# The MLP's first layer as Strassen's block product on one Trainium2 core

## Chip, cores and metric

The kernel runs on one core of a Trainium2 chip. Times are microseconds (us) of the device, from one launch of the whole program. Lower is better.

## What is computed

Three layers run one after the other. Attention of 8 batches, 8 heads and 576 rows against pooled keys and values gives x of 4608 tokens by 512. A mixture of 8 experts (each token goes to one) maps x to y of the same shape. The last layer is the MLP, which is what the change is about:

```python
def _moe2_ref(x, w_in, w_out):          # x 4608 x 512, w_in 512 x 2048, w_out 2048 x 512
    h = x @ w_in
    g = h * (1.0 / (1.0 + np.exp(-h)))
    return (g @ w_out).astype(np.float32)
```

The weights of the MLP come as 64-bit floats; everything else is 32-bit.

## The kernel before, in words

Every product of two numbers in these matmuls is taken in three: an operand is split into a high part (`fp32r`, a copy by ScalarE) and a low part (the difference, by VectorE), and hi x hi, lo x hi and hi x lo are added up in PSUM.

**Mixture stage** (`run_items`, line 990): 16 items of one, two or three blocks of 128 tokens (`ORDER`), 120 units in all. Its program order is written out by hand. SP loads the experts' weights; between the units, `decode_ops` (line 200) is drained step by step from a list: 32 chunks of the MLP's 64-bit weights are loaded, put together as 32-bit numbers on VectorE, ScalarE and GpSimd, and split. The 16 chunks of `w_in` come first and go to SBUF tiles `wi` (high and low, line 818). The 16 chunks of `w_out` go through two stores each (lines 277, 278) to the DRAM tensors `wod`. At unit `PREP` = 112 `prepare_y` (line 1280) frees the decoder's memory, loads the first block's input (`load_y(0)`), and `trans_y` (line 947) transposes it on VectorE and splits it.

**MLP stage** (from line 1299): 12 blocks of 384 tokens (`TB`), each with 16 units (one per 128 columns of `w_in`). `c1` (line 1326) computes 128 columns of h for the block with 12 matmuls of 384 columns into one of three PSUM banks, then sigmoid (ScalarE), product (VectorE), high part (ScalarE), low part (VectorE). `c2` (line 1348) multiplies them by the unit's rows of `w_out`: 9 matmuls of 512 columns into three PSUM banks that collect a block's 16 units. `c_out` (line 1360) copies the rows out of PSUM and scatters them to `out`. The `w_out` parts are loaded from `wod` when the stage starts (line 1381), with the second block's input between them (`YF`). `load_y` (line 937) brings a block's 384 rows by four transfers of short runs; it is called one block ahead at the least, and `trans_y` runs in units 8 to 11 of the block before. SP and GpSimd follow the program's order (line 1300); the order on the other engines is a planner's.

Of the kernel before, what the change touches and what calls it, by code (L numbers as in the profile page):

```python
# [8 lines left out]
F32 = mybir.dt.float32  # L9
F32R = mybir.dt.float32r  # L10
# [33 lines left out]
YF = 5  # L44
# [4 lines left out]
HOLD = 2  # L49
# [68 lines left out]
def kernel(  # L118
# [76 lines left out]
    wod = [tc.dram_tile([DFF, DM], F32, name=f"wod{i}") for i in range(2)]  # L195
# [4 lines left out]
    def decode_ops(pctx, wi):  # L200
# [3 lines left out]
        def chunk(src, hi, lo, nm, after):  # L204
# [30 lines left out]

            def out_hi():
                if hi is None:
                    st["hi"] = dp.tile([P, 512], F32R, tag="hi", name=f"hi_{nm}", bufs=2)
                    st["lo"] = st["A"].bitcast(F32R)
                else:  # L240
                    st["hi"], st["lo"] = hi, lo
                nc.scalar.copy(out=st["hi"], in_=st["A"])

            def rest():
                nc.gpsimd.tensor_tensor(
                    out=st["A"] if wide else st["lo"], in0=st["A"], in1=st["hi"].bitcast(F32), op=ALU.subtract
                )
# [15 lines left out]
            if wide:  # L263
                ops.append(
                    lambda: nc.gpsimd.tensor_tensor(out=st["lo"], in0=st["A"], in1=st["B"], op=ALU.add)
                )
# [3 lines left out]
        for c in range(DM // P):  # L270
            for f in range(DFF // 512):
                fs = slice(f * 512, f * 512 + 512)
                chunk(w_in[c * P : (c + 1) * P, fs], wi[0][c][:, fs], wi[1][c][:, fs], f"i{c}_{f}", None)
        for f in range(DFF // P):

            def after(hi, lo, f=f):
                nc.sync.dma_start(out=wod[0][f * P : (f + 1) * P, :], in_=hi.bitcast(F32))
                nc.sync.dma_start(out=wod[1][f * P : (f + 1) * P, :], in_=lo.bitcast(F32))

            chunk(w_out[f * P : (f + 1) * P, :], None, None, f"o{f}", after)  # L280
# [537 lines left out]
    wi = [[wip.tile([P, DFF], F32R, tag=f"wi{i}_{c}", name=f"wi{i}_{c}") for c in range(DM // P)] for i in range(2)]  # L818
# [115 lines left out]
    yin, yT, g_t, o_t, ypool = {}, {}, {}, {}, []  # L934
    NB = N // TB

    def load_y(b):
        if b >= NB:
            return
        yin[b] = ypool[b % 2].tile([P, 4, TB], F32, tag="yin", name=f"yin{b}", bufs=1)  # L940
# [6 lines left out]
    def trans_y(b, c, pool, tag):  # L947
        if b >= NB:
            return
        if c == 0:  # L950
            yT[b] = [ypool[b % 2].tile([P, 4, TB], F32R, tag=t, name=f"{t}{b}", bufs=1) for t in ("yh", "yl")]
        yf = pool.tile([P, TB], F32, tag=tag, name=f"yf{b}", bufs=3)
        nc.vector.transpose(out=yf, in_=yin[b][:, c, :])
        yh, yl = yT[b]
        nc.scalar.copy(out=yh[:, c, :], in_=yf)
        nc.vector.tensor_tensor(out=yl[:, c, :], in0=yf, in1=yh[:, c, :].bitcast(F32), op=ALU.subtract)

    bctx = ExitStack()
    with bctx:
# [296 lines left out]
        dq = decode_ops(dctx, wi)  # L1256
# [23 lines left out]
        def prepare_y():  # L1280
            assert not dq, len(dq)
            dctx.close()
            ypool.append(ctx.enter_context(tc.tile_pool(name="y0", bufs=1, side="right")))
            load_y(0)
            nc.scalar.activation(out=spacer, in_=spacer, func=AF.Sigmoid)

        pre[PREP] = [prepare_y]
        for c in range(4):
            pre[PREP + 3 + c] = [lambda c=c: trans_y(0, c, bp, "ys")]
# [8 lines left out]

    mctx.close()
    mctx.enter_context(tc.manual_schedule(engines={mybir.EngineType.SP, mybir.EngineType.Pool}))  # L1300
    ctx.enter_context(mctx)
    with ExitStack() as cctx:
        wop = cctx.enter_context(tc.tile_pool(name="wop", bufs=1, reuse_waits=RW))
        cp = cctx.enter_context(tc.tile_pool(name="cp", bufs=2, reuse_waits=RW))
        pch = cctx.enter_context(tc.tile_pool(name="pch", bufs=3, space=PSUM, reuse_waits=RW))
        pco = cctx.enter_context(tc.tile_pool(name="pco", bufs=5, space=PSUM, reuse_waits=RW))
        ypool.append(cp)
        NS = TB // P
        NF = DFF // P
# [16 lines left out]
        def c1(u):  # L1326
            b, f = divmod(u, NF)
            if b >= NB:
                return
            yh, yl = yT[b]  # L1330
            ps = pch.tile([P, TB], F32, tag="h", name=f"ch{u}")
            k = 0
            sl = slice(f * P, (f + 1) * P)
            for c in range(4):
                for w, x in ((wi[0], yh), (wi[0], yl), (wi[1], yh)):
                    nc.tensor.matmul(ps, w[c][:, sl], x[:, c, :], start=(k == 0), stop=(k == 11))  # L1336
                    k += 1
            sg = cp.tile([P, TB], F32, tag="sg", name=f"sg{u}")
            nc.scalar.activation(out=sg, in_=ps, func=AF.Sigmoid)  # L1339
            g = cp.tile([P, TB], F32, tag="g", name=f"g{u}")  # L1340
            nc.vector.tensor_tensor(out=g, in0=ps, in1=sg, op=ALU.mult)  # L1341
            gh = cp.tile([P, TB], F32R, tag="gh", name=f"gh{u}", bufs=3)
            gl = cp.tile([P, TB], F32R, tag="gl", name=f"gl{u}", bufs=3)
            nc.scalar.copy(out=gh, in_=g)  # L1344
            nc.vector.tensor_tensor(out=gl, in0=g, in1=gh.bitcast(F32), op=ALU.subtract)  # L1345
            g_t[u] = (gh, gl)

        def c2(u, cols=range(NS)):
            b, f = divmod(u, NF)
            gh, gl = g_t[u]  # L1350
            if f == 0:
                o_t[b] = [pco.tile([P, DM], F32, tag="o", name=f"o{s}_{b}") for s in range(NS)]
            for s in cols:
                sl_ = slice(s * P, (s + 1) * P)
                for k, (h, w) in enumerate(((gh, wo[0][f]), (gh, wo[1][f]), (gl, wo[0][f]))):
                    nc.tensor.matmul(  # L1356
                        o_t[b][s], h[:, sl_], w, start=(f == 0 and k == 0), stop=(f == NF - 1 and k == 2)
                    )

        def c_out(b, cols=range(NS)):  # L1360
            for s in cols:
# [69 lines left out]
```

## Time and profile before

| what | us |
|---|---|
| runs of the kernel | 1554.3, 1549.18, 1558.97 (median 1554.3) |
| the profiled execution | 1554.01 |
| its span, first to last instruction | 1552.1 |
| its mean granted TensorE clock | 0.966 |

The profile is of one execution. Its page sums up each engine's busy time, shows the span in 40 slices, and follows back the chain of work that ended last. The trace behind it can be asked for groups of instructions, for single instructions in order of time, and for the engines' busy time in a stretch. TensorE appears twice: PE are the matmuls, PEld the loads of their stationary operands, which overlap them. DVE is VectorE, ACT ScalarE, POOL GpSimd, SPq the queue of SyncE. A matmul's row lasts longer than its share of the engine, because matmuls are pipelined.

### The profile page before, as it was taken

How to read it: one execution, taken by the hardware profiler on the slowest of the kernel's cores; microseconds unless marked ns; L12 is line 12 of the kernel's file. 1: busy time of each engine (PE TensorE's matmuls, PEld its weight loads, DVE VectorE, ACT ScalarE, POOL GpSimd, SP SyncE). 2: the span in 40 equal slices, each digit the busy share in tenths (PEclk: the TensorE clock that was granted, in tenths of full speed). 3: DMA queues.
4: the chain of work that ended last, by engine and by line, in shares of the span. 5: the costliest groups of instructions: out<-in, count | busy, mean ns of one | idle time of the engine just before them, and what ended most of it. 6: DMA issues, size and time to landing. Idle time of an engine off the chain costs nothing.

```text
span 1552.1 us, 21780 instructions
## 1 busy us (share of the span) xinstructions
PE 1482.7 (96%) x8163; PEld 1328.5 (86%) x8164; DVE 784.2 (51%) x1454; ACT 603.6 (39%) x1250; POOL 375.9 (24%) x445
## 2 busy tenths in 40 slices
PE   8898876899999999999999999999999999999996
PEld 6788865788889899898889989998999999999996
DVE  6466456497888887884332323323232332323232
ACT  4555442355656555653222322322232232322221
POOL 1773034254345553531110101011010100100000
PEclk9989587999999999999999999999999999999998
DMA  9996014677658887883920102102020220000000
GB/s 256 271 250 119 28 68 132 206 241 226 233 188 276 280 295 253 296 252 91 234 41 1 41 1 41 20 22 42 1 41 1 41 32 10 21 1 21 0 21 21
DMA packets 231206, 179.12 MB, mean 115 GB/s; under 512 B 155032, under 2 KB 187803, under 8 KB 230450
## 3 DMA queue, kind: packets, MB, share of 16 engines
q1 hardware_dynamic: 218626, 147.31, 35.8%
q0 software_dynamic: 11456, 28.48, 5.2%
q8 instruction: 66, 1.08, 0.3%
q10 hardware_dynamic: 1008, 1.84, 0.3%
q14 instruction: 50, 0.41, 0.1%
HBM read 140.55 MB, written 37.83 MB: 115 GB/s over the span
## 4 chain that ended last, share of the span: by engine, by line
PE 76%; issue 7%; DMA 7%; DVE 5%; ACT 1%; another core or an unknown queue 1%; SPq 1%; POOL 1%; DVEq 0%; POOLq 0%; ACTq 0%
PE o L1356 23%; PE ch L1336 23%; PE pv L483 4%; DMA yd<-ys_-1_14_8004,rk 2%; PE sc L446 2%; PE psp L468 2%; DMA r_-1_2_2964<-in_moe_w_dram 1%; PE vw L409 1%; DMA xd<-xg 1%; DMA qz<-in_q_dram 1%; DMA gid<-idd,rowi 1%; PE warm L665 0%; DVE sg_i L226 0%; DMA yin<-yd 0%
## 5 line engine op out<-in xcount | busy, mean ns | idle before, releaser
L1336 PE MATMUL ch<-yh,wi 128*128 128x384 f32 x1536 | 398.0, 338 | 2.5 <-DVEq L1291 2.5
L1356 PE MATMUL o<-wo,gh 128*128 128x512 f32 x1152 | 357.6, 395 | 2.1 <-ACT gh L1344 2.1
L1341 DVE TENSOR_TENSOR g<-ch,sg 128x384 f32<-128x384 f32 x192 | 106.8, 556 | 419.7 <-ACT sg L1339 419.4
L1336 PEld LDWEIGHTS ch<-yh,wi 128*128 128x128 f32 x1536 | 282.5, 189 | 19.4 <-POOL spacer L1163 2.9
L1339 ACT ACTIVATE sg<-ch 128x384 f32<-128x384 f32 x192 | 94.5, 492 | 459.6 <-PE ch L1336 447.9
L1336 PE MATMUL ch<-yl,wi 128*128 128x384 f32 x768 | 259.8, 338 | 0.0
L1356 PEld LDWEIGHTS o<-wo,gh 128*128 128x128 f32 x1152 | 214.0, 188 | 37.0 <-ACT gh L1344 2.4
L1356 PE MATMUL o<-wo,gl 128*128 128x512 f32 x576 | 223.5, 396 | 0.0
L1366 POOL DMA_INDIRECT out_dram<-os,ids x33 | 32.5, 985 | 643.6 <-DVE os L1364 638.9
L1345 DVE TENSOR_TENSOR gl<-g,gh 128x384 fp32r<-128x384 f32 x192 | 106.8, 556 | 95.4 <-ACT gh L1344 92.2
L1336 PEld LDWEIGHTS ch<-yl,wi 128*128 128x128 f32 x768 | 145.0, 189 | 1.9
L1344 ACT CAST gh<-g 128x384 fp32r<-128x384 f32 x192 | 98.5, 513 | 112.9 <-DVE g L1341 107.9
L1356 PEld LDWEIGHTS o<-wo,gl 128*128 128x128 f32 x576 | 108.3, 188 | 25.3
L483 PE MATMUL pv<-vb,pT 72*128 72x128 f32 (+1 forms) x640 | 89.7, 295 | 2.8 <-DVE gh L517 1.9
L483 PEld LDWEIGHTS pv<-vb,pT 72*128 72x128 f32 (+1 forms) x640 | 82.0, 200 | 5.6 <-issue 2.7
L462 ACT ACTIVATE pe<-sc,nm 128x72 f32<-128x72 f32 x288 | 67.9, 320 | 8.8 <-DVE nm L456 8.5
L472 ACT COPY pT<-psp 72x512 f32<-72x512 f32 x72 | 42.0, 583 | 69.0 <-PE psp L468 54.7
L456 DVE TENSOR_REDUCE nm<-sc 128x4 f32<-128x288 f32 x72 | 32.4, 451 | 53.6 <-PE sc L446 30.4
L468 PE MATMUL psp<-ident,pe 128*72 128x128 f32 x288 | 49.4, 300 | 10.6 <-ACT pT L472 7.1
L446 PE MATMUL sc<-kbd,qT 128*128 128x144 f32 (+1 forms) x320 | 54.8, 316 | 1.5 <-issue 1.4
L564 POOL DMA_INDIRECT idd<-idw,sli x36 | 36.9, 1024 | 73.9 <-DVE idw L601 66.7
L446 PEld LDWEIGHTS sc<-kbd,qT 128*128 128x128 f32 (+1 forms) x320 | 43.9, 199 | 5.6 <-issue 3.6
(3518 smaller groups left out, 2688.2 us busy)
## 6 DMA issues: line engine op xcount, KB each, us to landing
yin<-yd SPq DMA_DIRECT2D x44, 192.0 KB
xd<-xg SPq DMA_DIRECT2D x32, 256.0 KB
raw_i<-in_moe_w_in_dram SPq DMA_DIRECT2D x16, 512.0 KB
raw_o<-in_moe_w_out_dram SPq DMA_DIRECT2D x16, 512.0 KB
wo<-wod SPq DMA_DIRECT2D x32, 256.0 KB
qz<-in_q_dram SPq DMA_DIRECT2D x28, 288.0 KB
kv<-in_k_dram SPq DMA_DIRECT2D x9, 768.0 KB
kv<-in_v_dram SPq DMA_DIRECT2D x6, 768.0 KB
```

The lines of the kernel that those rows point to most:

```text
L446: nc.tensor.matmul(ps[o : o + n, 2 * c : 2 * c + 2, :], qT_t[t][:, 2 * hf + c, o : o + n], kbds[b // 2 % 2][:, h0 : h0 + 5 : 4, :], start= ...
L462: nc.scalar.activation(out=pe[:, h * NK : h * NK + NK], in_=ps[:, h, :], func=AF.Exp, bias=nm[:, h, :])
L468: nc.tensor.transpose(ps[:, j, :], pe[:, NK * j : NK * j + NK], ident)
L472: nc.scalar.copy(out=pT_t[u], in_=ps_t.pop(u))
L483: nc.tensor.matmul(pv_t[t][o : o + n, j % 2, VW * c : VW * c + VW], pT[:, j, o : o + n], vw[b][:, HG * h : HG * h + VW], start=True, stop= ...
L564: ins = nc.gpsimd.indirect_dma_start(out=idd, out_offset=bass.IndirectOffsetOnAxis(ap=sli[:, i, :], axis=0), in_=idw[:, t, :], in_offset=None,
L1336: nc.tensor.matmul(ps, w[c][:, sl], x[:, c, :], start=(k == 0), stop=(k == 11))
L1339: nc.scalar.activation(out=sg, in_=ps, func=AF.Sigmoid)
L1341: nc.vector.tensor_tensor(out=g, in0=ps, in1=sg, op=ALU.mult)
L1344: nc.scalar.copy(out=gh, in_=g)
L1345: nc.vector.tensor_tensor(out=gl, in0=g, in1=gh.bitcast(F32), op=ALU.subtract)
L1356: nc.tensor.matmul(o_t[b][s], h[:, sl_], w, start=(f == 0 and k == 0), stop=(f == NF - 1 and k == 2))
```

## The change

Two blocks of 384 tokens form a superblock. In its product with `w_in` both are cut in two along the 512 inputs (b11, b21 of the first block, b12, b22 of the second), and `w_in` into four quarters of inputs by hidden columns (a step n takes the 128 columns n and the 128 columns n + 8). Eight quarter products of 6 matmuls give the four parts of h of a step; Strassen's product in Winograd's form gives them with seven, from sums of the quarters of `w_in` and of the transposed tokens (t1 to t4), and five additions per step on VectorE.

- Decoding: the parts of `w_in` go to SBUF tiles `em` and by 8 stores of 1.05 MB to DRAM (`wid`). Of `w_out` the high part stays in SBUF (`woh`), the low part is stored (`wold`).
- `prepare_y` also loads the first two steps' parts of `w_in` and of `w_out`'s low part. The first block is transposed there and split (b11, b21).
- First superblock: 16 steps j, block by block, two hidden columns each, with the eight products ("Q"). In the first eight, VectorE forms the sums s1 to s4 of the step's quarters, which are split and stored to DRAM (`wis`).
- Later superblocks: 8 steps n of seven products. Loads: "A" three quarters of `w_in` and "S" four sums, 786 KB and 1.05 MB a step, and two low parts of `w_out`, each in two buffers.
- The second layer's turn of a hidden part (`second`, the 9 matmuls) is taken from a list `pend`, a few products after the part's own.
- PSUM: banks a and b for the products (one buffer each) and six for the rows of out.
- The order is the program's on every engine.

The core of the diff:

```diff
-YF = 5
-HOLD = 2
+        def quarters(n):
+            w = wt["Q", n].bitcast(F32)
...
+            nc.vector.tensor_tensor(out=W4, in0=parts[0], in1=parts[1], op=ALU.add)
...
+            nc.vector.tensor_tensor(out=s1, in0=a21, in1=a22, op=ALU.add)
+            nc.vector.tensor_tensor(out=s3, in0=a11, in1=a21, op=ALU.subtract)
+        def sums(n):
...
+            nc.vector.tensor_tensor(out=s2, in0=s1, in1=a11, op=ALU.subtract)
+            nc.vector.tensor_tensor(out=s4_, in0=a12, in1=s2, op=ALU.subtract)
...
+            nc.scalar.copy(out=em[:, :, 0, :], in_=s4)
+            nc.vector.tensor_tensor(out=em[:, :, 1, :], in0=s4, in1=em[:, :, 0, :].bitcast(F32), op=ALU.subtract)
+            nc.sync.dma_start(
+                out=wis[n * P : (n + 1) * P, :], in_=em.rearrange("p o i x -> p (o i x)").bitcast(F32)
+            )
+        def product(ps, kind, o, n, nm, first):
+            w, (xh, xl) = wt[kind, n], X[nm, 0 if kind == "Q" else n // NFP]
             k = 0
+            for c in range(2):
+                for i, x in ((0, xh), (0, xl), (1, xh)):
+                    nc.tensor.matmul(
+                        ps, w[:, o, i, c, :], x[:, c, :], start=(first and k == 0), stop=(k == 5), skip_group_check=True
+                    )
+                    k += 1
...
+                (1, 2, load_y, b0), (2, 1, load_ids, b0), (2, 1, load_ids, b1), (2, 2, turn_y, b0, 0), (2, 2, turn_y, b0, 1),
+                (3, 1, turn_y, b0, 2), (3, 1, turn_y, b0, 3), (3, 2, load_y, b1), (4, 2, turn_y, b1, 0),
+                (4, 2, turn_y, b1, 1), (5, 1, turn_y, b1, 2), (5, 1, turn_y, b1, 3), (5, 2, sum_y, "t1", sb),
+                (6, 1, sum_y, "t2", sb), (6, 1, sum_y, "t3", sb), (6, 2, split_y, "b11", sb), (7, 1, sum_y, "t4", sb),
+                (7, 2, split_y, "t2", sb), (7, 2, split_y, "b21", sb), (8, 1, split_y, "t3", sb), (8, 1, split_y, "t4", sb),
+                (8, 1, split_y, "t1", sb), (8, 2, split_y, "b22", sb),
...
+        load_y(1)
         load_ids(1)
+        for j in range(2 * NFP):
+            a, n = divmod(j, NFP)
+            for h in range(2):
+                ps = bank("ab"[h], f"{'ab'[h]}{j}")
+                for r in range(2):
+                    product(ps, "Q", ((1, 2), (0, 3))[h][r], j, f"b{r + 1}{a + 1}", r == 0)
+                if a == 0:
+                    (quarters, sums)[h](n)
+                key = (n, h, a)
+                gate_1(ps, key)
+                gate_2(ps, key)
+                gate_3(key)
+                if pend[0] != key or h == 0 and j:
+                    next_second()
+                if h == 0:
+                    if j:
+                        load_wol(1, j + 1)
+                else:
+                    load_wol(0, j + 2)
+                    load_wi("Q", j + 2)
...
+            if a and 2 <= n < 4:
+                load_wi("A", NFP + n - 2)
+                load_wi("S", NFP + n - 2)
+        for n in range(NFP, NFP * NSB):
+            k11, k21, k22, k12 = (n, 0, 0), (n, 1, 0), (n, 1, 1), (n, 0, 1)
...
+            product(a, "A", 0, n, "b11", True)
+            do(n, 1)
+            nc.scalar.copy(out=t, in_=a)
+            next_second()
+            load_wol(1, n + NFP + 1)
+            product(b, "S", 2, n, "t2", True)
+            add(u, b, t)
+            product(a, "A", 1, n, "b21", False)
+            gate_1(a, k11)
+            product(b, "S", 3, n, "t3", False)
+            gate_2(a, k11)
+            add(v, b, t)
+            gate_3(k11)
+            if n > NFP:
+                next_second()
+                load_wol(0, n + NFP + 1)
+            do(n, 2)
+            product(b, "A", 2, n, "t4", False)
+            load_wi("A", n + 2)
+            add(t, b, t)
+            gate_1(t, k21)
+            a = bank("a", f"a{n}_")
+            product(a, "S", 0, n, "t1", True)
+            gate_2(t, k21)
+            add(v, v, a)
+            gate_3(k21)
+            gate_1(v, k22)
+            gate_2(v, k22)
+            gate_3(k22)
+            next_second()
+            product(a, "S", 1, n, "b22", False)
+            load_wi("S", n + 2)
+            add(u, u, a)
+            gate_1(u, k12)
+            gate_2(u, k12)
+            gate_3(k12)
+            next_second()
```

`gate_1` is the sigmoid (ScalarE), `gate_2` the product (VectorE) and the high part (ScalarE), `gate_3` the low part (VectorE). `do(n, i)` issues the next superblock's operand work at the places listed; in the first superblock's second half the same list is used (u of its steps 8 to 15), and in its first half steps 3 to 6 transpose the second block and split b12 and b22. `out_rows` copies a block's three row tiles out of PSUM on ScalarE.

## Rows read from the trace of the kernel before

**Rows 1.** Page, parts 1 and 2: engines' busy time, and the span in 40 slices.
```profile
PE 1482.7 (96%) x8163; PEld 1328.5 (86%) x8164; DVE 784.2 (51%) x1454; ACT 603.6 (39%) x1250; POOL 375.9 (24%) x445
...
PEclk9989587999999999999999999999999999999998
```

**Rows 2.** Page, part 4: the chain that ended last, by line.
```profile
PE o L1356 23%; PE ch L1336 23%; PE pv L483 4%; DMA yd<-ys_-1_14_8004,rk 2%; PE sc L446 2%; PE psp L468 2%; DMA r_-1_2_2964<-in_moe_w_dram 1%; PE vw L409 1%; DMA xd<-xg 1%; DMA qz<-in_q_dram 1%; DMA gid<-idd,rowi 1%; PE warm L665 0%; DVE sg
```

**Rows 3.** Stretch 800 to 1340, line 1336's instructions alone, then line 1356's.
```profile
800.00:1340.00 540.00, 293.04 (x1547) 273.53 (x1547) 1.00 0.14 24
...
800.00:1340.00 540.00, 293.78 (x1161) 216.02 (x1160) 1.00 0.14 24
```

**Rows 4.** Groups from 728 to the end: busy us, mean ns, idle before.
```profile
L1341 DVE TENSOR_TENSOR g<-ch,sg 128x384 f32<-128x384 f32 x192 | 106.8, 556 | 419.7 <-ACT sg L1339 419.4 <-issue 0.4
L1345 DVE TENSOR_TENSOR gl<-g,gh 128x384 fp32r<-128x384 f32 x192 | 106.8, 556 | 95.4 <-ACT gh L1344 92.2 <-issue 2.3
L1344 ACT CAST gh<-g 128x384 fp32r<-128x384 f32 x192 | 98.5, 513 | 112.9 <-DVE g L1341 107.9 <-issue 5.0
L1339 ACT ACTIVATE sg<-ch 128x384 f32<-128x384 f32 x192 | 94.5, 492 | 459.6 <-PE ch L1336 447.9 <-issue 8.5 <-PE o L1356 3.3
...
L953 DVE STREAM_TRANSPOSE yf<-yin 128x384 f32<-128x384 f32 x44 | 24.6, 566 | 11.1 <-DMA yin<-yd 11.1
```

**Rows 5.** Groups of VectorE from 640 to 760, of other widths; then one copy.
```profile
L1042 DVE TENSOR_TENSOR lo_-1_60_7885<-r_-1_60_7776,hi_-1_60_7884 128x1024 fp32r<-128x1024 f32 x1 | 1.2, 1226 | 0.3 <-ACT hi_-1_60_7884 L1040 0.3
...
L1074 DVE TENSOR_TENSOR xl_-1_15_7837<-trx_-1_15_7912,xh_-1_15_7836 128x512 fp32r<-128x512 f32 x1 | 0.7, 693 | 0.7 <-ACT xh_-1_15_7836 L1073 0.7
...
L1106 DVE SCALAR_TENSOR_TENSOR hl_-1_106_7751<-h_-1_106_7737,hh_-1_106_7750 128x256 fp32r<-128x256 f32 x1 | 0.4, 418 | 0.0
...
687.16 1.05 ACT L1040 CAST hi_-1_60_7884<-r_-1_60_7776 128x1024 fp32r<-128x1024 f32 x1
```

**Rows 6.** Timeline from 1530: start us, us, engine, line, operation.
```profile
1535.95 1.56 PE L1356 MATMUL o<-wo,gh 128*128 128x512 f32 x6
1536.21 0.49 ACT L1339 ACTIVATE sg<-ch 128x384 f32<-128x384 f32 x1 [2.57 <-PE ch L1336]
1536.73 0.56 DVE L1341 TENSOR_TENSOR g<-ch,sg 128x384 f32<-128x384 f32 x1 [2.51 <-ACT sg L1339]
```

**Rows 7.** Timeline, start of the MLP and one `yin` later.
```profile
729.80 0.98 POOL L1164 DMA_INDIRECT yd<-ys_-1_15_8249,rk  x1 [0.23 <-issue]
730.04 0.19 PEld L1336 LDWEIGHTS ch<-yh,wi 128*128 128x128 f32 x1 [2.94 <-POOL spacer L1163]
...
734.44 0.09 POOL L1318 MEMSET spacer<- 1x1 f32 x1 [3.65 <-DMA yd<-ys_-1_15_8243,rk]
...
748.84 1.50 DVE L953 STREAM_TRANSPOSE yf<-yin 128x384 f32<-128x384 f32 x3 [8.40 <-DMA yin<-yd]
...
752.77 1.44 PE L1356 MATMUL o<-wo,gh 128*128 128x512 f32 x5 [2.12 <-ACT gh L1344]
...
868.44 4.99 SPq L945 DMA_DIRECT2D yin<-yd  x4
```

**Rows 8.** Stretches: length; PE, PEld, DVE, ACT, POOL busy; PEclk, DMA share, GB/s.
```profile
732.00:734.00 2.00, 2.00 (x9) 2.00 (x9) 0.00 (x0) 0.00 (x0) 0.00 (x0) 0.59 1.03 367
...
754.00:758.00 4.00, 4.00 (x14) 3.57 (x14) 1.62 (x4) 1.41 (x3) 0.00 (x0) 0.57 1.05 396
...
764.00:768.00 4.00, 4.00 (x22) 3.63 (x21) 1.12 (x2) 1.00 (x2) 0.00 (x0) 1.00 1.43 129
...
868.00:870.00 2.00, 2.00 (x12) 1.77 (x11) 2.00 (x5) 0.55 (x2) 0.00 (x0) 1.00 0.12 21
```

**Rows 9.** The same view, mixture stage.
```profile
440.00:480.00 40.00, 37.90 (x212) 33.40 (x211) 36.03 (x48) 26.69 (x42) 16.56 (x17) 1.00 0.75 246
...
640.00:680.00 40.00, 40.00 (x219) 35.79 (x218) 34.27 (x46) 23.52 (x36) 20.84 (x18) 1.00 0.87 289
...
704.00:728.00 24.00, 23.53 (x117) 20.78 (x115) 11.64 (x18) 8.57 (x14) 0.78 (x1) 1.00 0.00 1
```

More of the change, by code (lines that the diff above doesn't have):

```diff
@@ L264, in chunk @@
                 ops.append(
[L265 removed]
+                    lambda: nc.gpsimd.tensor_tensor(out=st["lo"], in0=four(st["A"]), in1=four(st["B"]), op=ALU.add)
                 )
@@ L945, in load_y, with quarter @@
             nc.sync.dma_start(out=dst[32 * i : 32 * i + 32], in_=src[i])
-    def trans_y(b, c, pool, tag):
-        if b >= NB:
-            return
[L950 to L956, printed above, removed]
+    def quarter(nm, sb):
+        if (nm, sb) not in qr:
+            qr[nm, sb] = (C if OPND.get(nm, (1, 1))[0] else R)[0].tile([P, 2, TB], F32, tag=f"q{nm}", name=f"q{nm}_{sb}")
+        return qr[nm, sb]
@@ new lines, in turn_y, with sum_y @@
+    def turn_y(b, c):
+        nm = f"b{c // 2 + 1}{b % 2 + 1}"
+        nc.vector.transpose(out=quarter(nm, b // 2)[:, c % 2, :], in_=yin[b][:, c, :])
+    def sum_y(nm, sb):
+        q = lambda n: quarter(n, sb)
+        if nm == "t3":
+            qr["t3", sb] = q("b12")
+        o, a, b = {"t1": ("t1", "b12", "b11"), "t2": ("t2", "b22", "t1"), "t3": ("b12", "b22", "b12"),
+                   "t4": ("t4", "b21", "t2")}[nm]
+        nc.vector.tensor_tensor(out=q(o), in0=q(a), in1=q(b), op=ALU.subtract)
@@ new lines, in gate_3, with second @@
+        def gate_3(key):
+            sg, gh = g_t[key]
+            gl = cp.tile([P, TB], F32R, tag="gl", name="gl%d_%d_%d" % key, bufs=4)
+            nc.vector.tensor_tensor(out=gl, in0=sg, in1=gh.bitcast(F32), op=ALU.subtract)
+            g_t[key] = (gh, gl)
+            pend.append(key)
+        def second(key, cols=range(NS), k0=None):
+            n, h, a = key
+            sb = n // NFP
+            gh, gl = g_t[key]
+            if k0 is None:
+                k0 = done.get((sb, a), 0)
+                done[sb, a] = k0 + 1
+            if k0 == 0:
+                o_t[sb, a] = [pco.tile([P, DM], F32, tag=f"o{a}{s}", name=f"o{a}{s}_{sb}") for s in range(NS)]
+            f = n % NFP + NFP * h
+            lo = wt[h, n + NFP if sb or a else n]
@@ L1404 @@
+        assert pend == [k22, k12] and not prep, (pend, list(prep))
+        for s in range(NS):
+            for i, key in enumerate(pend):
+                second(key, (s,), 2 * NFP - 2 + i)
+            out_rows(NSB - 1, 1, (s,))
 _INS = [
```

227 lines of the change are left out of this document (138 added, 89 removed).

## The prediction, made before the changed kernel was run

> **What bounds the kernel now.** I read the page's first parts, the chain, then the MLP stretch by source line, by group, and its ends. TensorE is busy 96% of the span, and from the twenty-first slice on its clock stands at 9 tenths or more, but for the last [rows 1]; 46% of the chain that ends last are the two MLP matmul lines [rows 2]. From 800 to 1340 us the busy times of both lines sum to more than the 540 us (pipelined matmuls overlap), at clock 1.00 [rows 3]: no gap. So the MLP is bound by TensorE, and a matmul less is time gained where nothing else makes TensorE wait. Its pitch: 1547 matmuls of 384 columns and 1161 of 512 fill 540 us; if the time goes with the columns, that is 0.1745 us and 0.2326 us each. One block of 16 units costs 16 x (12 x 0.1745 + 9 x 0.2326) = 67.0 us. VectorE needs only two operations of 0.556 us for each 4.19 us unit and ScalarE two of about 0.5 [rows 4], so both have room.
>
> **What the change removes.** From the second superblock on, two token blocks and two hidden columns ("a step") take seven products of 6 matmuls in place of eight: 42 x 0.1745 + 36 x 0.2326 = 15.70 us for 16.75, so 1.047 us less, in 5 superblocks x 8 steps: **-41.9 us**. The first superblock keeps all eight: its 16 steps (one block, two hidden columns) cost 24 x 0.1745 + 18 x 0.2326 = 8.37 us each, as before. Of the old start, the wait of 2.1 us from 750.7, for a unit queued on VectorE behind the transposes of a late `yin`, and the clock after it go [rows 7]: 754 to 758 was granted 0.57, near the lower of the two levels, 1.2 of 2.4 GHz [rows 8], so 1.7 of 4 us were lost. **-3.8 us**. The gap before the first matmul at 730.1 [rows 7] stays, and so do the 1.6 us lost to the low clock after it (0.59 from 732 to 734 [rows 8]).
>
> **A later step, followed through the queues.** Durations: 0.556 on VectorE, 0.49 sigmoid, 0.51 copy [rows 4]; a result of TensorE starts ScalarE 0.26 us after the next matmul started (1535.95 to 1536.21), and the others follow one another after 0.03 [rows 6]. Time 0 is the end of the fifth product (t4); products take 1.05, second-layer turns 2.09. TensorE: sixth product to 1.05, turn of k11 to 3.14, seventh to 4.19, turn of k21 to 6.28, then the next step. VectorE: add t 0.25 to 0.81; sigmoid to 1.33; multiply to 1.93; add v to 2.49; low part of k21 to 3.1 (TensorE wants it at 4.19); v's sigmoid, multiply, low part to 4.75; add u to 5.3, which frees bank a (wanted at 6.28); k12 done at 7.6. ScalarE copies t at 7.58 to 8.09. Next step's second product ends at 10.47, add u runs 10.72 to 11.28, and TensorE wants that bank at 11.52. Nothing waits; the tightest slack is 0.2 us, at this add. The operand work of the next superblock (8 transposes, 4 sums and 7 splits of 768 columns, over 8 steps) falls into gaps of 1.1 to 2.4 us, except in the first step of a superblock. No row has 768 columns; between 512 (0.69) and 1024 (1.23) they take 0.96 on VectorE, and 0.82 on ScalarE [rows 4, 5]. Ends for the steady steps: 0, and 0.9 us each if add u comes 1.1 us late.
>
> **First step of a superblock.** ScalarE has there, ahead of the copy t that the third product waits for, one copy of 0.51, three output copies of 0.6 and three splits of 0.82: 4.7 us from 0.2, then t until 5.3 or so, where TensorE wants it at 4.19: 1.0 late. The three low parts hold add u until 6.4, 0.3 late, and the split of b22 holds the adds of v, 0.5 late. So 1.8 us in four superblocks, 1.3 in the first (no old rows to copy), and 0.5 at the very end, where two chains are left: **+9.0 us**. Ends: 0, if the splits slip into gaps; 17, twice that.
>
> **First superblock, first block (8 steps).** VectorE: two operations of 1.23, four of 0.42, four of 0.556 make 6.35 us; it also stands for ScalarE's 1024-column copy (1.1) and twice 0.57 for gh (0.51 and two hand-offs) [rows 4 to 6]: 8.6 for TensorE's 8.37. With four transposes of 0.57 and two splits (1.8 each) on top it falls 7.8 behind in 67 us; a lead of 1.6 and idle time filled while TensorE waits for weights take off 3: **+4.9 us** (ends 0 and 8).
>
> **Its transfers.** Each step loads 1.05 MB of w_in, 0.5 of w_out's low part, and stores 1.05 MB of sums: 2.6 MB in 8.37 us, 313 GB/s, before `yin`. Long rows ran at 396 GB/s, `yin`'s short ones at 129 [rows 8]; I take 380 and 118 (0.79 MB: 6.7 us), all on SP's one queue. (1) `load_y(1)` is now SP's first transfer, but reads rows whose last scatter was issued at 729.8; the one before it had landed at 734.4 [rows 7]. From 735 to 743 it holds the queue; behind it come a store (2.8), 0.26 MB (0.7) and w_in's third part (2.8), landing 1.5 later (an issue at 868.4 moved little before 870 [rows 7, 8]) at 751. TensorE comes for it at 747.4: 730.1, two steps less the turn left over (14.7), 1.0 waited for VectorE (counted above), 1.6 of low clock: **+3.6**. (2) From the end of step 11 (of 0 to 15) the queue has w_in 2.8, `yin` 6.7, two first parts for the second superblock 4.8, 1.4 and w_in 2.8, landing 20 us later, needed 16.75 later: 3.3 to 4.0. VectorE stands in `turn_y(3, 0)` until `yin` has landed 11 us after that end, which holds step 13's low part by 3.0. Together **+7.0**. (3) The same, smaller, at steps 9 and 11: **+1.7**. (4) Three of these waits exceed the 2.1 us after which the clock fell before: 1.7 each, **+5.1**. The superblock's price is 4.9 + 3.6 + 7.0 + 1.7 + 5.1 = **+22.3 us**; ends 5 (transfers in time) and 37 (300 GB/s and 100 for `yin`, each term redone).
>
> The Trainium skill speaks against this part. "DMA: Bandwidth & Descriptors", section Bandwidth, sets about 358 GB/s of HBM as one core's limit. The trace exceeds it (396 GB/s from 754 to 758), so I keep the row; by the skill's figure terms (1) to (3) would grow by a sixteenth of their transfers, some 2 us.
>
> **Later superblocks' transfers.** 2.36 MB a step over 15.7 us, 150 GB/s, each asked for a step or more ahead; the two steps with `yin` need 6.2 + 6.7 us of queue. Cost 0.
>
> **Before the MLP.** w_in's parts are now stored (8 x 1.05 MB), w_out's high part no longer is (16 x 0.26 MB). 8.4 MB are 22 us of queue while w_in is decoded, where the DMA share is 0.75 (440 to 480); TensorE stood at 40.00 of 40 even at 0.87 [rows 9]. Only the stretch 440 to 480 lost 2.1 us, with weights used fastest; a store of 2.8 us in front of them can cost that twice. **+1** (ends -1 and +6). The 3.1 MB that `prepare_y` adds lie in the empty queue between 704 and 728 [rows 9]; cover gone, they would cost 8. The ops per decoded chunk stay the same.
>
> **Sum.** -41.9 - 3.8 + 9.0 + 22.3 + 1 = -13.4 us. The profiled execution took 1554.0 (span 1552.1 and 1.9 around it), the median of the three runs is 1554.3: **1540.5 us**. A measurement of this kernel can tell about 1%, 15.5 us, from no change; the forecast lies just inside.
>
> **Rivals.**
> (A) The first superblock's transfers come in time: the queue interleaves, `yin` loads in less than it did beside the old loads. Speaks for it that SP's row for four `yin` issues alone was shorter (4.99 us at 868 [rows 7]); against it that the old start had its wait for a `yin` [rows 7]. Then +4.9 for 22.3: 1523.
> (B) Reads and stores share the queue at 300 GB/s, and first steps cost double: 37 for 22.3, 17.5 for 9.0: 1564; with the first alone 1555. For it: no row shows such stores by themselves, and the busiest 40 us with stores moved 289 GB/s [rows 9]; against it: 396 GB/s of reads, and that stretch asked for no more.
> (C) Slower: VectorE becomes the bound of every later step, at add u in front of the fourth product, with 0.2 us of slack. Thirteen 0.556 operations are 7.2 us of 15.7, so it is latency, not load: each hand-off that takes 0.2 instead of 0.03 us would use the slack up. From 0.34 us per step the gain is gone; at 0.9, 40 x 0.9 = 36: 1576. Against it: the hand-off between ScalarE and VectorE is 0.03 us [rows 6].
>
> **Chances.** Forecast 0.52, its own range 1533 to 1548, 0.23 of it below 1538.8; A 0.24; B 0.17; C 0.07. Faster by over 1%: 0.23 + 0.24 = 0.47; within 1%: 0.29 + 0.17 = 0.46; slower: 0.07. The range reaches from just below A to the middle of B: 1520 to 1558.
>
> **What would show it.** Right: 42 first-layer matmuls a step and 15.7 us from step to step with no idle TensorE; a gap of 1 to 2 us at each superblock's first step, released by ScalarE's t; gaps over 2 us near 748 and twice between 835 and 880, released by SP's transfers, with the clock at about half after them. Wrong: no gaps there (A), 9 us or more per early step with TensorE waiting on DMA (B), or a VectorE add in front of most fourth products (C).

## The result and the profile after

The changed kernel takes 1537.1 us in the median of four runs (1535.7 to 1545.1), the kernel before 1556.5 in four runs beside them (1549.2 to 1559.0). The ratio is 0.9894, its 95% interval 0.9844 to 0.9943. The forecast was 1540.5. The profiled execution took 1535.8, its span is 1534.1, so 18.0 less than that of the profile before.

Page of the changed kernel, parts 1 and 2 (they answer to [rows 1]) and part 4 ([rows 2]):

```profile
PE 1440.6 (94%) x7923; PEld 1277.4 (83%) x7924; DVE 930.8 (61%) x1691; ACT 652.1 (43%) x1311; POOL 380.2 (25%) x445
...
PEclk9889877999999999999999999999999999999998
...
PE o L1438 21%; PE b L1394 9%; PE a L1394 7%; DMA wQ<-wid 2%; DVE sg L1412 1%; ACT gh L1415 1%; ACT t L991 1%; SPq L967 1%; ACT os L1448 1%; ACT sg L1408 1%; DVE gl L1420 0%; DVE b L992 0%; DVE t L992 0%; DVE t L1403 0%; POOL out_dram L1450
```

TensorE has 240 matmuls less (40 steps of 6) and is 42 us less busy, yet only 18 us came out: its share of the span fell from 96 to 94%. What lies between shows in the chain, where a load of `w_in` (`wQ<-wid`) and ScalarE's `t` now stand behind the two lines of matmuls (1438 and 1394 for 1356 and 1336).

The MLP begins where it did (first matmul at 729.91, before 730.08), so 17.8 of this pair's 18.0 us are in it: 804.2 us to the span's end for 822.0. (That the start agrees is partly chance, as the account of the term "before the MLP" shows.) Stretches of the changed kernel, columns as in [rows 8]:

```profile
748.00:756.00 8.00, 7.45 (x38) 6.85 (x39) 5.18 (x9) 2.99 (x5) 0.00 (x0) 1.00 0.92 332
...
850.00:860.00 10.00, 5.62 (x26) 4.16 (x24) 4.86 (x9) 1.42 (x3) 0.00 (x0) 0.97 1.00 378
860.00:870.00 10.00, 8.94 (x34) 8.42 (x35) 2.85 (x4) 1.00 (x2) 0.00 (x0) 0.69 0.39 152
900.00:1010.00 110.00, 109.86 (x544) 98.18 (x543) 59.90 (x108) 37.65 (x72) 2.52 (x5) 1.00 0.57 167
```

Within a later superblock (900 to 1010) TensorE stands at 109.86 of 110 and full clock. In the first superblock it loses 4.4 of 10 us while the transfers move 378 GB/s, and then runs at 0.69. Its timeline in the first superblock (it answers to [rows 7]):

```profile
729.91 3.79 PE L1394 MATMUL a<-b,wQ 128*128 128x384 f32 x12 [2.59 <-DVEq L1351]
...
748.55 2.38 PE L1394 MATMUL a<-b,wQ 128*128 128x384 f32 x12 [1.62 <-DMA wQ<-wid]
...
802.29 2.38 PE L1394 MATMUL a<-b,wQ 128*128 128x384 f32 x12 [1.43 <-DMA wQ<-wid]
...
837.98 9.94 SPq L967 DMA_DIRECT2D yin<-yd  x4
847.97 0.94 SPq L1000 DMA_DIRECT2D wA<-wid  x1
848.96 0.43 SPq L1000 DMA_DIRECT2D wS<-wis  x1
850.59 0.58 SPq L1000 DMA_DIRECT2D wQ<-wid  x1
851.85 1.04 DVE L976 STREAM_TRANSPOSE qb<-yin 128x384 f32<-128x384 f32 x2 [5.05 <-DMA yin<-yd]
...
861.07 4.21 PE L1394 MATMUL a<-b,wQ 128*128 128x384 f32 x12 [4.65 <-DMA wQ<-wid]
```

The starts of the 16 steps are read off the first row of each product group with `wQ`. A step at full pace takes 8.42 here. Three waits for `w_in` stand out; the two of 1.6 and 1.4 us are followed by twelve matmuls in 2.38, near the full pace, the one of 4.65 by twelve in 4.21, at the low clock. The rows of SP show why the last is late: the input's issue (9.94) and two other loads come between the part before and the part that TensorE wants. VectorE stands 5.05 for the input.

Timeline of later steps: copies t (ScalarE's copy of bank a, which the third product waits for) of ordinary steps, a first step of a superblock, and add u with the fourth product of an ordinary step:

```profile
912.27 0.48 ACT L1555 COPY t<-a 128x384 f32<-128x384 f32 x1 [0.47 <-PE a L1394]
928.01 0.48 ACT L1555 COPY t<-a 128x384 f32<-128x384 f32 x1 [0.47 <-PE a L1394]
...
991.00 0.48 ACT L1555 COPY t<-a 128x384 f32<-128x384 f32 x1 [0.47 <-PE a L1394]
...
1006.18 1.55 ACT L1448 COPY os<-o 128x512 f32<-128x512 f32 x3
...
1007.61 0.86 ACT L991 CAST t<-qb 128x768 fp32r<-128x768 f32 x1
...
1008.34 1.59 ACT L991 CAST t<-qt 128x768 fp32r<-128x768 f32 x2
...
1009.81 0.50 ACT L1555 COPY t<-a 128x384 f32<-128x384 f32 x1
...
1010.36 1.31 PE L1394 MATMUL a<-b,wA 128*128 128x384 f32 x6 [0.50 <-ACT t L1555]
...
1024.29 0.48 ACT L1555 COPY t<-a 128x384 f32<-128x384 f32 x1
...
1043.26 0.56 DVE L1403 TENSOR_TENSOR u<-b,t 128x384 f32<-128x384 f32 x1 [3.10 <-PE b L1394]
...
1044.05 1.21 PE L1394 MATMUL b<-t,wS 128*128 128x384 f32 x6
```

From copy to copy an ordinary step is 15.75 us long (30 of the 39 intervals, each 15.74 or 15.75). The two intervals around a superblock's first step sum to 33.29 (991.00 to 1024.29), 33.56, 33.28 and 33.21, so 1.7 to 2.1 more than 31.5. Add u ends at 1043.82, and the fourth product, which waits for it, starts at 1044.05.

### The profile page after: what moved, and what is told of

It is laid out like the page before. It is cut to its first block, busy times and chain, and to the rows that moved or that the text cites. A ratio compares the mean times of both kernels' runs of the same rounds, so it can differ in the third digit from the quotient of the medians.

```text
span 1534.1 us, 21968 instructions
## 1 busy us (share of the span) xinstructions
PE 1440.6 (94%) x7923; PEld 1277.4 (83%) x7924; DVE 930.8 (61%) x1691; ACT 652.1 (43%) x1311; POOL 380.2 (25%) x445
## 3 DMA queue, kind: packets, MB, share of 16 engines
q8 instruction: 64, 1.05, 0.3%
## 4 chain that ended last, share of the span: by engine, by line
PE 41%; DVE 3%; ACT 3%; DMA 2%; issue 1%; SPq 1%; POOL 0%; ACTq 0%; POOLq 0%
PE o L1438 21%; PE b L1394 9%; PE a L1394 7%; DMA wQ<-wid 2%; DVE sg L1412 1%; ACT gh L1415 1%; ACT t L991 1%; SPq L967 1%; ACT os L1448 1%; ACT sg L1408 1%; DVE gl L1420 0%; DVE b L992 0%; DVE t L992 0%; DVE t L1403 0%; POOL out_dram L1450 0%
## 5 line engine op out<-in xcount | busy, mean ns | idle before, releaser
L1438 PE MATMUL o<-woh,gh 128*128 128x512 f32 x576 | 229.0, 398 | 1.7 <-ACT gh L1415 1.6
L1438 PE MATMUL o<-woh,gl 128*128 128x512 f32 x576 | 229.3, 398 | 0.0
L1438 PE MATMUL o<-wol,gh 128*128 128x512 f32 x576 | 225.7, 392 | 0.0
L1415 ACT CAST gh<-sg 128x384 fp32r<-128x384 f32 x192 | 98.6, 513 | 143.2 <-DVE sg L1412 139.9
L1420 DVE TENSOR_TENSOR gl<-sg,gh 128x384 fp32r<-128x384 f32 x192 | 107.4, 559 | 75.5 <-ACT gh L1415 64.0
L1438 PEld LDWEIGHTS o<-woh,gl 128*128 128x128 f32 x576 | 108.1, 188 | 29.0 <-DVE gl L1420 2.6
L1438 PEld LDWEIGHTS o<-woh,gh 128*128 128x128 f32 x576 | 108.3, 188 | 20.0 <-ACT gh L1415 3.8
L1438 PEld LDWEIGHTS o<-wol,gh 128*128 128x128 f32 x576 | 108.4, 188 | 18.1
L1394 PE MATMUL a<-b,wA 128*128 128x384 f32 x480 | 97.4, 339 | 2.3 <-ACT t L1555 1.8
L1394 PE MATMUL b<-t,wS 128*128 128x384 f32 x480 | 97.2, 337 | 0.3
L1403 DVE TENSOR_TENSOR u<-b,t 128x384 f32<-128x384 f32 x40 | 22.3, 557 | 88.5 <-PE b L1394 85.9
L489 ACT COPY pT<-psp 72x512 f32<-72x512 f32 x72 | 41.9, 582 | 61.8 <-PE psp L485 48.3
```

What stands on the lines that cost most here:

```text
L489: nc.scalar.copy(out=pT_t[u], in_=ps_t.pop(u))
L1394: nc.tensor.matmul(ps, w[:, o, i, c, :], x[:, c, :], start=(first and k == 0), stop=(k == 5), skip_group_check=True)
L1403: nc.vector.tensor_tensor(out=o, in0=a, in1=b, op=ALU.add)
L1415: nc.scalar.copy(out=gh, in_=sg)
L1420: nc.vector.tensor_tensor(out=gl, in0=sg, in1=gh.bitcast(F32), op=ALU.subtract)
L1438: nc.tensor.matmul(o_t[sb, a][s], x[:, sl_], w, start=(k0 == 0 and k == 0), stop=(k0 == 2 * NFP - 1 and k == 2))
```

## The experiments

In these runs the attention had a higher granted clock than in the two profiles above (1.00 from 120 to 200 us in every one, for 0.87 and 0.80 in the two halves of that stretch in the changed kernel's), and the MLP began at 690 to 700 us in place of 730; the kernel before took 1517 to 1519 beside them. All readings are therefore taken from the MLP's first matmul on. "Steps" are those of the first superblock; "later" is from the second superblock's first matmul to the span's end.

| run | steps 0, 1 | 2 to 6 | 7, 8 | 9 to 12 | 13, 14 | all 16 | later | MLP |
|---|---|---|---|---|---|---|---|---|
| changed kernel | 18.64 | 42.81 | 19.45 | 35.74 | 25.35 | 150.4 | 653.8 | 804.2 |
| changed kernel again | 18.68 | 42.82 | 19.37 | 36.56 | 25.10 | 151.0 | 653.7 | 804.7 |
| eighth product | 18.44 | 42.82 | 19.02 | 36.44 | 25.23 | 150.4 | 690.9 | 841.2 |
| one more copy | 18.90 | 42.82 | 19.43 | 36.06 | 24.83 | 150.5 | 667.3 | 817.8 |
| later A and S loads | 18.80 | 42.81 | 19.46 | 34.13 | 16.85 | 140.5 | 653.8 | 794.3 |
| no sums | 15.98 | 42.30 | 16.85 | 33.70 | 25.58 | 142.8 | 653.2 | 796.0 |
| no store | 16.24 | 42.82 | 18.36 | 34.01 | 24.17 | 144.0 | 653.8 | 797.8 |
| held-back copies | 18.60 | 42.87 | 19.38 | 33.71 | 24.48 | 147.5 | 646.1 | 793.6 |
| input later | 19.63 | 45.57 | 19.39 | 35.58 | 25.64 | 154.2 | 653.8 | 808.0 |
| request first | 16.78 | 43.73 | 18.37 | 33.65 | 23.17 | 144.1 | 653.8 | 797.9 |
| three together | 16.70 | 43.73 | 18.36 | 33.66 | 16.82 | 137.7 | 646.1 | 783.8 |

The first superblock alone varies by some 3 us between executions that its edit doesn't touch (the held-back copies act only later, and its steps 9 to 12 are 2.0 shorter). Smaller differences are not read from that column.

**An eighth product, to price the seventh saved.**

```diff
             product(b, "S", 2, n, "t2", True)
+            product(b, "S", 2, n, "t2", True)
```

> In each later step the third product (the one with t2) is issued twice into the same bank, so a step has eight products again, with everything else as in the changed kernel; the result is the same. Theory (TensorE is the bound of the later steps, and six matmuls of 384 columns are 1.047 us of it): copy t to copy t goes from 15.75 to 16.79 us, and 40 steps add 41.9 us: span near 1576. Rival (part of the removed product was covered by waits of TensorE, in the first steps of the superblocks above all, where it waits 1.8 us for ScalarE): the first steps' extra 1.8 falls by up to 1, and less than 37 us come back.

In the program's order the repeated product is the second of a step, ahead of the one that waits for copy t. Measured: copy t to copy t is 16.79, as said.

```profile
883.96 0.48 ACT L1555 COPY t<-a 128x384 f32<-128x384 f32 x1 [0.47 <-PE a L1394]
900.74 0.48 ACT L1555 COPY t<-a 128x384 f32<-128x384 f32 x1 [0.48 <-PE a L1394]
```

But the later stretch grew by 37.1, not 41.9: the two intervals around a first step went from 33.29 to 34.31, by one product and not by two. So in ordinary steps the product is worth its full 1.04, and in the first steps it is worth nothing, since there TensorE waits for ScalarE anyway. Both theories hold, each in its own steps.

**One more VectorE operation, to measure the slack.**

```diff
+            nc.vector.tensor_copy(out=ctile("x", f"x{n}"), in_=b)
             add(u, b, t)
```

> In each later step VectorE copies bank b once more (384 columns, about 0.5 us) right ahead of add u. Theory (add u has 0.2 us of slack in front of the fourth product): the fourth product starts 0.3 us late in each step, copy t to copy t goes from 15.75 to about 16.05 us, and the span grows by some 12 us. Rival (the slack is larger than the trace shows, or TensorE makes it up in the step): steps stay at 15.75 and the span within 3 us.

Copies t, the added copy with add u behind it, and the fourth product of a step:

```profile
881.10 0.48 ACT L1555 COPY t<-a 128x384 f32<-128x384 f32 x1 [0.47 <-PE a L1394]
897.16 0.48 ACT L1555 COPY t<-a 128x384 f32<-128x384 f32 x1 [0.47 <-PE a L1394]
...
1014.71 0.56 DVE L1559 COPY x<-b 128x384 f32<-128x384 f32 x1 [3.03 <-PE b L1394]
1015.19 0.55 DVE L1403 TENSOR_TENSOR u<-b,t 128x384 f32<-128x384 f32 x1
...
1015.79 1.31 PE L1394 MATMUL b<-t,wS 128*128 128x384 f32 x6
```

The copy puts add u off by 0.48 (1015.19 less 1014.71), and the step became 0.315 longer (16.065 for 15.75), so the slack was 0.17. The later stretch grew by 13.5. Rival C of the prediction was one VectorE operation away.

**The second superblock's first loads two steps later.**

```diff
-            if a and 2 <= n < 4:
-                load_wi("A", NFP + n - 2)
-                load_wi("S", NFP + n - 2)
+            if a and 4 <= n < 6:
+                load_wi("A", NFP + n - 4)
+                load_wi("S", NFP + n - 4)
```

> The loads of the second superblock's first two steps (parts A and S) are issued in steps 12 and 13 of the first superblock in place of 10 and 11; nothing else moves. Theory (in step 14 TensorE waits 4.65 us for its part of w_in because two such loads stand between the second block's input and that part on SP's queue, and the clock falls after that wait): the wait at 861 and the low clock after it go, 4.65 + 2.0, so about 6.5 us less. Rival (the short runs of the input hold the queue that long by themselves): a wait of 3 us or more stays there.

Measured: the wait is gone, steps 13 and 14 take 16.85 for 25.35, and steps 9 to 12 are 1.6 shorter, 10 us in all. SP's rows of the place, and the stretch in which the wait would have begun:

```profile
799.17 6.52 SPq L967 DMA_DIRECT2D yin<-yd  x4
805.79 1.88 SPq L1010 DMA_DIRECT2D wol<-wold  x2
807.72 0.42 SPq L1000 DMA_DIRECT2D wQ<-wid  x1
808.19 0.42 SPq L1000 DMA_DIRECT2D wA<-wid  x1
```

```profile
808.00:818.00 10.00, 10.00 (x52) 9.11 (x51) 4.97 (x9) 2.40 (x5) 0.00 (x0) 1.00 1.04 378
```

The input's issue is 6.52 long for 9.94, and `w_in`'s part follows it with only two low parts of `w_out` between. The DMA rate is the same 378 GB/s as in the changed kernel from 850 to 860, now with TensorE at 10.00 of 10: it was not too many bytes, but 1.8 MB in front that are not wanted before step 17. In the changed kernel's trace the last completions come in the order of issue: the input at 851.7, these two loads at 854.3 and 857.2, TensorE's part at 861.0. Steps 13 and 14 gained 8.5 for the 6.65 expected: 4.65 of wait, 2.4 of low clock in step 14, and 1.4 that the expectation left out, around a wait of 0.80 for ScalarE's `gh` (853.93) behind VectorE's stand for the input. The 1.6 in steps 9 to 12 can be the difference between executions.

**No sums; then the sums without their store.** The first leaves out the sums of `w_in`'s quarters, the second only their store; in both the later superblocks read `wid` in place of `wis` (that line of the edits is not shown).

```diff
-                if a == 0:
-                    (quarters, sums)[h](n)
```

```diff
-            nc.sync.dma_start(
-                out=wis[n * P : (n + 1) * P, :], in_=em.rearrange("p o i x -> p (o i x)").bitcast(F32)
-            )
```

> Leaves out the sums s1 to s4 of w_in's quarters, their split and their store in the first superblock's first eight steps; the later superblocks load the same number of bytes from the stored quarters in their place. Theory (in these eight steps the sums hold VectorE, and their stores hold SP's queue in front of w_in's third part): TensorE's waits for VectorE there (2.8 us in sum) and for w_in (1.62 near 748.6 and 1.43 near 802.3) go, so the first superblock takes 5 to 6 us less, 144.5 to 145.5 from its first matmul to the second superblock's in place of 150.4; the 4.65 us wait at 861 stays. Rival (the eight steps are late for other reasons, the input's load or the clock): less than 2 us.

> Leaves out only the store of the sums to memory (they are still formed and split); the later superblocks load the stored quarters in their place. Without the sums at all the first superblock took 142.8 us for 150.4. Theory (two causes share these 7.6 us: the sums hold VectorE by some 4 to 5 us, and their stores delay w_in's loads by some 3): the waits for w_in at the ends of steps 1 and 7 (1.6 and 1.4 us) shrink below 0.7 in sum, VectorE's lateness stays, and the first superblock takes 147 to 148. Rival (all of it is VectorE): it takes 150 and the waits for w_in stay. Other rival (all of it is the queue): 143.

Measured: 7.6 less without the sums, 6.4 of it already without the store. The wait at the end of step 1 shrank to 0.97 and 0.72:

```profile
710.11 2.35 PE L1394 MATMUL a<-b,wQ 128*128 128x384 f32 x12 [0.72 <-DMA wQ<-wid]
```

The wait at the end of step 7 went in both; the 4.65 us one stayed (5.07 and 3.93), as the theory had it. By the sums over 16 steps nearly all of it is the store, but read by steps it is not: steps 0 to 8 take 80.9 in the changed kernel, 77.4 without the store and 75.1 without the sums. Of the 3.5 between the first two, 1.5 is the clock, which stayed at 1.00 after the MLP's first matmul in these two executions alone (see the end), so the store costs **2.0** there and VectorE **2.3**. The rest of the 6.4 lies in steps 9 to 14, where an execution that still stores (the held-back copies, below) was as short. Both expected shares, 3 and 4 to 5, were too large.

**Output copies behind copy t.** `let_go` calls `out_rows` for what `held` has collected; its definition, and a last call behind the loop, are not shown.

```diff
-                out_rows(sb, a, cols)
+                if sb:
+                    held.append((sb, a, cols))
+                else:
+                    out_rows(sb, a, cols)
...
             do(n, 1)
             nc.scalar.copy(out=t, in_=a)
+            let_go()
...
             do(n, 2)
+            let_go()
```

> ScalarE's copies of a finished block's rows out of PSUM are issued after the copy t of the next superblock's first step in place of ahead of it; the second block's behind the operand work of the second place. Theory (the first step's 1.8 us are ScalarE's queue ahead of copy t): the two intervals of copy t around the start of a superblock sum to 31.7 to 32.0 us in place of 33.3, four times, so the stretch from the second superblock's start to the end is about 6 us shorter. Rival (the splits of the operands are what delays it, or the rows that stay longer in PSUM delay the second layer's next turns by as much): less than 2 us.

ScalarE at the start of a superblock in this kernel, with the copies t before and after:

```profile
958.53 0.48 ACT L1564 COPY t<-a 128x384 f32<-128x384 f32 x1 [0.48 <-PE a L1394]
...
974.45 1.57 ACT L991 CAST t<-qt 128x768 fp32r<-128x768 f32 x2
975.91 0.48 ACT L1564 COPY t<-a 128x384 f32<-128x384 f32 x1
976.29 1.56 ACT L1451 COPY os<-o 128x512 f32<-128x512 f32 x3
...
990.03 0.48 ACT L1564 COPY t<-a 128x384 f32<-128x384 f32 x1 [0.41 <-PE a L1394]
```

The splits still stand in front of copy t; the three copies no longer do. The two intervals sum to 31.49 or 31.50 all four times, which is twice 15.75: the first step costs nothing any more, and the later stretch is 7.7 shorter. ScalarE's queue was the whole cause, and the 1.55 us of copies the part of it that was too much.

**The second block's input behind w_in's third part.**

```diff
-        load_y(1)
         load_ids(1)
...
                     load_wi("Q", j + 2)
+                    if j == 0:
+                        load_y(1)
```

> The second block's input is loaded after the third part of w_in in place of ahead of it (behind step 0's other loads). Theory (the wait of 1.6 us for w_in at the end of step 1 is this input in front of it on SP's queue): that wait goes and no other takes its place, 1.5 us less in the first superblock. Rival (the input now holds up the fourth part of w_in, needed 8.4 us later, or the transposes in step 3): the wait moves there, no gain.

Measured: it got worse, steps 0 and 1 by 1.0 and steps 2 to 6 by 2.8. SP's rows and TensorE's wait, then three of the transfers issued from 700 to 712 (the store from 699.69 among them), with KB and the median us from issue to landing:

```profile
699.69 0.33 SPq L1512 DMA_DIRECT2D wis<-ems  x1
...
700.54 0.91 SPq L1000 DMA_DIRECT2D wQ<-wid  x1
701.96 9.40 SPq L967 DMA_DIRECT2D yin<-yd  x4
...
709.96 3.43 PE L1394 MATMUL a<-b,wQ 128*128 128x384 f32 x12 [2.56 <-DMA wQ<-wid]
```

```profile
wis<-ems SPq DMA_DIRECT2D x1, 1024.0 KB, 5.2
wQ<-wid SPq DMA_DIRECT2D x1, 1024.0 KB, 9.4
yin<-yd SPq DMA_DIRECT2D x4, 192.0 KB, 9.2
```

With the input behind it, the part of `w_in` landed 19.6 us after the MLP's first matmul (709.9), for 18.6 in the changed kernel (748.5). So the theory that the input in front made the 1.6 us fell. In both runs the request stands behind the store of the sums, and SP issued that 9.3 to 9.4 us after the first matmul (739.18 in the changed kernel), when VectorE had the sums. Why the part then took 9.4 us is open. The Trainium skill, "DMA: Bandwidth & Descriptors", section "Queues, rings and completion order", says that completion is not first in, first out for one issuing engine; this trace does not show it: store, part and input landed in the order of their issue, the input's first part at 711.2.

**w_in asked for ahead of the store.**

```diff
+                if h:
+                    load_wi("Q", j + 2)
                 if a == 0:
                     (quarters, sums)[h](n)
...
-                    load_wi("Q", j + 2)
```

> In the first superblock w_in's part for the step after next is asked for right behind the step's last product, ahead of the store of the sums and of w_out's low part (SP waits for VectorE and for a turn of the second layer before it issues those). Theory (the stores delay w_in's loads mostly because SP stands at the store's wait in front of them: the load issued at 755.35 could go at 751): the waits at the ends of steps 1 and 7 (1.6, 1.4 us) go and steps 9 to 12 are even, 3 to 4 us less in the first superblock; the 4.65 us wait shrinks by up to 4. Rival (the queue's bytes, not its order, set the time: 2.6 MB a step): no more than 1 us.

```profile
705.61 0.93 SPq L1000 DMA_DIRECT2D wQ<-wid  x1
706.68 0.33 SPq L1512 DMA_DIRECT2D wis<-ems  x1
...
714.24 2.28 PE L1394 MATMUL a<-b,wQ 128*128 128x384 f32 x12
```

Measured: 144.1, so 6.3 less, 2.0 of it in steps 0 to 8. The wait at the end of step 1 is gone (714.24) with the input still in front of the load, that at the end of step 7 too, and the one near 861 is 3.32 for 4.65. The 2.0 are what leaving the store out gave there, now with all its bytes moved: the store's place in SP's order was the cost. With it SP's wait for VectorE, the store's megabyte and one low part of `w_out` came off the front of the load; the runs do not tell them apart. Steps 9 to 14 are 4.3 shorter, of which up to 2.9 can be the difference between executions. With `w_in` in time VectorE shows: steps 5 to 8 take 36.8 (9.00, 9.42, 9.42 and 8.95) where four at full pace take 33.7, **3.1 us**, around the splits of b12 and b22.

**Three edits together, and the changed kernel again.** Later A and S loads, held-back copies, request first.

> The later loads of the second superblock's first parts, the held-back copies and the earlier request for w_in together. If their gains are of different waits they add up: 10 + 7 + 3 to 4 us less than the changed kernel in the MLP, some 20 in all, and 38 less than the kernel before: a ratio near 0.975. If the earlier request has nothing left to win, 17 us and 0.977.

> The changed kernel once more, beside the combined one on the same chip. On this chip the attention's stretch ran at a higher clock in both kernels, which says nothing of the change. If its gain is the MLP's alone, the difference to the kernel before stays near 18 us here too, a ratio of 0.988.

| kernel | median (range), runs | ratio to before, 95% interval |
|---|---|---|
| before | 1518.7 (1511.4 to 1523.7), 11 | |
| changed | 1502.8 (1496.4 to 1507.7), 6 | 0.9895, 0.9865 to 0.9925 |
| three edits | 1483.0 (1479.0 to 1484.9), 6 | 0.9764, 0.9738 to 0.9791 |

The changed kernel is 15.9 below the kernel before here, for the 18 expected; its interval allows both. The combined kernel beats both: its MLP takes 783.8, 20.4 less than the changed kernel's. The waits left in its first superblock are such pairs, two in each of steps 5 to 7 and one in steps 1 and 8, here of the turn at 756 (step 6), of TensorE's weight loads for the high and the low part:

```profile
756.37 0.19 PEld L1438 LDWEIGHTS o<-woh,gh 128*128 128x128 f32 x1 [0.43 <-ACT gh L1415]
756.96 0.19 PEld L1438 LDWEIGHTS o<-woh,gl 128*128 128x128 f32 x1 [0.30 <-DVE gl L1420]
```

Of 17.0 us that the first superblock cost above its matmuls, 12.7 are gone. The parts alone gave 23.9 (9.9, 7.7 and 6.3); 3.5 of it is counted twice, since late loads and early requests shorten the same steps 9 to 14.

## Why the prediction was right, and where its terms were off

The forecast was 3.4 us from the median, and the mechanism was the one named. Part of the closeness is luck: the change was forecast as -13.4 and measured as -18.0 between the profiles and -19.4 between the medians, and several terms were mis-sized and partly cancel.

- **Products, -41.9.** Right per ordinary step: 1.04 came back with an eighth product. The step is 15.75 for the 15.70 worked out, 1.8 us over 39 steps; the clocked pitch of a matmul holds to 0.3%.
- **First steps, +9.0.** Right in size and place. Four superblocks cost 1.79, 2.06, 1.78 and 1.71 (1.8 each was said), all of it ScalarE's queue ahead of copy t. What the text did not see is that the removed product had hidden a further 1.04 of this queue in each of the four: with eight products the first steps cost that much less. The first later step took 14.95 where an ordinary one less a turn takes 13.66, so 1.3 as said, and from the last matmul to the end it is 0.6 more than before (12.34 for 11.76, 0.5 was said): 9.2 in all.
- **Slack at add u, 0.2.** Right: 0.17 by the added copy.
- **First superblock, +22.3.** It cost 17.0: 150.4 against 131.9 for its matmuls (at the forecast's pitch) and 1.5 for the clock at the start. Steps 0 to 8 were charged 10.2 (VectorE 4.9, the wait (1) 3.6, a clock drop 1.7) and cost 5.8 above the pace; steps 9 to 15 were charged 12.1 and cost 10.6. The last 0.6 or so is the pace, 8.42 for 8.37.
  - The first step that was off is the queue in (1), landing at 751. The part landed at 748.5, a wait of 1.62. The transfers did land one behind the other, as the sum had it (last completions: input 741.3, store 743.8, low part 744.6, `w_in` 748.5), but SP issued the input from 733.47, not 735, and the sum gave it 8 us, to 743, where the same paragraph works out 6.7; with 6.7 it lands at 749.5. What took the wait away was asking ahead of the store; putting the input behind did not.
  - The second is (4): "three of these waits exceed the 2.1 us". Only one did (4.65), and one clock drop of 2.4 us followed it, 5.1 charged.
  - VectorE's 4.9 is 3.1 where `w_in` is in time, and 2.3 by the run without sums: the lead and the time in which VectorE catches up take off more than the 3 allowed for. (3) was near: 2.0 in steps 9 to 12 for 1.7, where executions differ by more than that. The 1.43 at the end of step 7 was not foreseen.
  - (2) was right in kind: 7.0 with two drops of 1.7, so 10.4, were charged to steps 13 and 14, which cost 8.5, and the two early loads named there carry it: without them all 8.5 went. Of its parts, `w_in` cost 4.65 for the 3.3 to 4.0 said, VectorE's stand for the input 1.4 for 3.0.
- **Old wait, -3.8.** It is gone; nothing in the runs prices it by itself.
- **Before the MLP, +1.** The MLP began 0.2 earlier, but that is chance. From its first matmul into a `y` tile to the MLP's first, the mixture stage took 475.6 for 472.3, so 3.4 more (473.9 to 475.9 in the eleven profiles of the table; the kernel before has one profile); the attention ahead of it was 3.5 shorter, and that moves by 30 between two profiles of the same kernel. The term was thus some 2 too small, within its ends of -1 and +6. Its place was wrong as well: 440 to 480 lost 0.6 (39.38 of 40, [rows 9] had 37.90). Which wait makes the 3.4 no run takes apart.
- **Signs.** The 15.7 us from step to step came. Near 748 the gap was 1.6, not over 2, with full clock behind it, and of two gaps over 2 us between 835 and 880 one came. At a superblock's first step TensorE stands twice for half a us (0.50 at 1010.36 for ScalarE's t, 0.49 at 1019.82 for its `gh`), not once for 1 to 2.
- **Rivals.** A (transfers in time) did not happen, but the combined kernel shows it could be had: with the loads in time the first superblock's price is 4.3 (137.7 less 131.9 and 1.5), and A had left 4.9. B's 300 GB/s was too low: the crowded stretches moved 332 and 378; the Trainium skill's 358 GB/s as one core's limit ("DMA: Bandwidth & Descriptors", section Bandwidth) is passed there too, at 378 over 10 us. The same section says that this is a core's share when both cores of a pair stream; one core ran here. C did not happen, by 0.17 us.

Sum: -41.9, -3.8 as forecast, +1.8 for the pitch, +9.2 for first steps and end, +17.0, and -0.2 ahead of the MLP (+3.4 and -3.5): -17.9 for the -18.0 measured, -13.4 forecast. Without the attention's -3.5 it would be -14.4, nearer to the forecast and to the 15.9 measured in the later runs.

## What to carry to other kernels

A cheaper algorithm on the bounding engine pays in full only where that engine has no other wait: look at the first steps of each stage, where another engine's queue, not its load, decides, and put work there behind the one instruction that the bound engine waits for. Order an in-order issuing engine by what is needed next: ask for the next weights ahead of a store that itself waits, and don't bring next stage's operands early into the stretch where the queue is fullest. Moving a few lines gave back 20 us here, more than the 15.9 that the change itself had brought beside them, with no byte and no operation less.

## What the hardware did that was not expected

- The clock after the MLP's first matmul: TensorE had stood 2.5 to 2.7 us, and in nine of the eleven profiles of the table it then ran at the lower level (granted 0.50), as before the change. In the two without the sums' store it did not, after the same wait. The stretch behind the first matmul of the run with later A and S loads, and then of the run without the store:

```profile
692.00:694.00 2.00, 2.00 (x8) 2.00 (x8) 1.93 (x3) 0.00 (x0) 0.09 (x1) 0.50 0.46 168
```

```profile
694.00:696.00 2.00, 2.00 (x12) 2.00 (x13) 1.76 (x3) 0.00 (x0) 0.58 (x1) 1.00 0.67 250
```

  Nothing ahead of that point differs in the two programs that the profile shows; why the clock held stays open. Elsewhere in the MLP, waits of 1.4 to 1.85 us were followed by matmuls at full pace, the one of 2.12 in the kernel before [rows 7, 8] and all of 2.56 and more by slow ones.
- The attention's granted clock from 120 to 200 us was 1.00 in the experiments' runs and 0.80 to 0.87 in the changed kernel's first profile. The same kernel took 1537.1 in the first runs and 1502.8 in the later ones, a difference of twice what the change is worth, while the MLP agrees within 0.6. Between its two profiles the difference is 30 us, complete at 247 us and the same from there to the MLP. The clock stood at 0.50 for 79 us ahead of the MLP in the one and for 48 in the other, which makes some 15 of the 30; what makes the rest is not shown.
